# Block attention and a top-1 mixture of experts on one core: value products from three 16-bit passes, gate products by batch

## The chip, the cores and the metric

One of the eight cores of a Trainium2 chip runs the whole kernel. The metric is device time in microseconds; a kernel is run several times and the median counts. The profile is taken in one execution.

## The reference

```python
# q, k, v: (8, 8, 576, 64) f32; 8 batches x 8 heads, 576 tokens, 64 per head
scores = (1/sqrt(64)) * q @ k.T                  # per batch and head
scores = where(pos_i // 64 >= pos_j // 64, scores, -1e9)
attn = exp(scores - max(scores)); attn /= sum(attn) + 1e-9
x = (attn @ v) as (4608 tokens, 512)             # heads side by side
logits = x @ w_gate                              # 8 experts
e = argmax(logits); gate = softmax(logits)[e]; eom = sigmoid(x @ w_output_gate)[e]
out[token] = gate * eom * (relu(x @ w1[e]) @ w2[e])   # w1 (512, 1024), w2 (1024, 512)
```

All results are f32. The choice of the expert hangs on small differences of the logits, so the attention has to be close to f32.

## The kernel before, in words

**Two stages.** The attention goes through 32 pairs of heads (8 batches, 4 pairs each). Its output x goes to DRAM, and after each batch a routing step writes each token's number and weight into a table sorted by expert. The experts' stage then takes groups of up to 256 tokens of one expert: gather x, two layers with w1 and w2 (each number split into two 16-bit parts, three products), scale, scatter to the output.

**One pair.** A class `Pair` has a method for each step; here with their lines.
- `fetch` (L103) loads q and k of both heads into `nat`. `split` (L109, L110) makes of each the upper f16 part and the f16 rest, in two pieces of 320 and 256 elements: the cast is on POOL for k and on ACT for q, the rest on POOL. `turn` (L118) transposes by DMA into `tr`. `highs` copies the upper parts into `kx` and `qx` (L122, L123, both DVE), 64 x 1152 each. `fetch_v` loads V (L129, L130) as f32 into `vf`, with a column of ones behind the 64 columns, so that the value product gives the sum of the probabilities too.
- `max_tile` 0 to 3: scores from upper parts alone, into a double PSUM bank, and their maximum over keys on DVE (L150 for tiles 0 and 1, L155 for 2 and 3; L158 writes them scaled as f16).
- `turn_max`: five transposes (L164), an ACT copy of the maxima into `qx` for the first head (L165), a DVE copy of that for the second (L166).
- `prob_tile` 0 to 3: scores in full, keys on partitions (L176, L177), maximum subtracted by the product itself; ACT takes the exponential (L189) into `pt`, f32, 2304 elements a partition in all.
- `values` 0 and 1, one head each: 15 f32 products of a 128x128 block of `pt` (the stationary operand) with 65 columns of `vf` (L207); then DVE adds 1e-9, inverts and scales (L209 to L211), and two DMAs store x (L216, L217).
- `turn_x`: five f32 transposes (L222, L226), two ACT copies to `xT` (L223, L227). `logits`: five f32 products with the 16 gate columns (L234), added to `L` on DVE (L237, L239).

**Order.** The order of PE is written by hand. Round g = 4p + r issues for r = 0 `max_tile(0)`, `prob_tile(2)` and `turn_x`; for r = 1 `turn_max`, `max_tile(1)`, `prob_tile(3)`, `logits`; for r = 2 and 3 `values(0)` or `values(1)`, then a `prob_tile` and a `max_tile`, each of the pair whose turn it is: probabilities run one pair behind the maxima, values two, x three. A table of events by round issues the loads and splits some rounds ahead (`make` 12, `split` 9 and 8, `turn` 7 and 6, `highs` 3 rounds ahead of the pair's first tile). Other engines take their instructions in an order that the scheduler fixes beforehand, by priority; each engine's queue is worked off in order. All DMAs but the gathers, scatters and table accesses go through SP's queue.

**Routing.** `finish_batch` (L394 to L443) is a generator that goes one step on in each round: the one-hot choice, its rank by products with triangular ones (L408 to L413), softmax and sigmoid on DVE and ACT, the product `z` on POOL (L436), five scatters into the table (L443, POOL). After the last pair, `first_tiles` fills PE with the first expert's products while this runs, one block of 12 products per step; then `route_rest` computes the groups of all other tokens. The first expert's weights are loaded and split on ACT and POOL (`load_first`, L657, L659) during the last pairs.

**PSUM.** Eight banks: `ps_s`, three double banks, for scores; `ps_o`, two single ones, for everything else.

Of the kernel before, what the change touches and what calls it, by code (L numbers as in the profile page):

```python
# [26 lines left out]
def block_attention_top1_moe(  # L27
# [44 lines left out]
    NSET = 4  # L72

# [3 lines left out]
    ps_o = ctx.enter_context(tc.tile_pool(name="ps_o", bufs=2, space=PSUM))  # L77
# [8 lines left out]

    def bank():
        return ps_o.tile([P, 512], F32, name="ps_o")

    class Pair:  # L90
# [22 lines left out]
        def room(self, which):  # L113
            self.tr[which] = sb.tile([P, NR, P], F16, name=f"tr{which}", bufs=5)
            return self.tr[which]
# [4 lines left out]
        def highs(self):  # L120
            self.trk, self.trq = (self.tr[i].rearrange("c r p -> c (r p)") for i in range(2))
            nc.vector.tensor_copy(self.kx[0:64], self.trk[0:64])  # L122
            nc.vector.tensor_copy(self.qx[0:64], self.trq[64:128])  # L123

        def fetch_v(self):
            h0 = 2 * self.hp
            self.v = vfs[self.p % len(vfs)]
            for h in range(2):
                nc.sync.dma_start(self.v[:, h, 0:4, 0:D], v[self.b, h0 + h, 0:512].rearrange("(j p) d -> p j d", p=P))  # L129
            nc.sync.dma_start(self.v[64:128, :, 4, 0:D], v[self.b, h0:h0 + 2, 512:576, :].rearrange("h p d -> p h d"))  # L130

        def max_tile(self, i):
            if i == 0:
                self.nmx = small.tile([P, NT, 2], F32, name="nmx")
            ps = ps_s.tile([P, 2, 512], F32, name="ps_s")
# [7 lines left out]
            if i < 2:  # L143
# [5 lines left out]
                for t, sl in zip(ts, cols):  # L149
                    last_max[0] = nc.vector.tensor_reduce(self.nmx[:, t, :], ps[:, :, sl], AX.X, ALU.max, negate=True)  # L150
            else:
# [3 lines left out]
                last_max[0] = nc.vector.tensor_reduce(self.nmx[:, 4, ab:ab + 1], flat[:, 0:S], AX.X, ALU.max, negate=True)  # L155
            if i == 3:
                self.nmz = nmzs[self.p % 2]
                nc.vector.tensor_scalar(self.nmz[:, :, 96:98], self.nmx, 1.0 / MS, None, ALU.mult)  # L158

        def turn_max(self):  # L160
            pm = ps_o.tile([P, 1024], F16, name="ps_o")
            for t in range(NT):
                at = QS[t] - (64 if 0 < t < 4 else 0)
                nc.tensor.transpose(pm[:, at:at + P], self.nmz[:, t, :], ident16)  # L164
            nc.scalar.copy(self.qx[96:98, 0:S], pm[96:98, 0:S])  # L165
            nc.vector.tensor_copy(self.qx[96:98, S:2 * S], self.qx[96:98, 0:S])  # L166

        def prob_tile(self, i):
            if i == 0:
                self.pt = [sb.tile([P, 2, n], F32, name=f"pt{j}") for j, n in enumerate((S, 512, 512))]  # L170
            ps = ps_s.tile([P, 2, 512], F32, name="ps_s")
# [7 lines left out]
            if i < 2:  # L179
                for ab in range(2):  # L180
                    for o, k0, q0 in (((0, 320), 256, 256), ((320, 512), 384, 384)) if i == 0 else (((0, 448), 128, 128), ((448, 512), 448, 512)):
                        products(ps[:, ab, o[0]:o[1]], ab, k0, q0, o[1] - o[0])
                to, ap = self.pt[2 - i], ps
            else:
                ab = i - 2
                products(flat[:, 0:512], ab, 0, 0, 512)
                products(flat[:, 512:S], ab, 0, 512, 64)
                to, ap = self.pt[0][:, ab], flat[:, 0:S]
            last_exp[0] = nc.scalar.activation(to, ap, AF.Exp, scale=SCALE)  # L189

        def values(self, ab):
            if ab == 0:
                self.xn = sb.tile([P, NT, P], F32, name="xn", bufs=3)
            o = bank()[:, 0:NT * (D + 1)].rearrange("p (t c) -> p t c", c=D + 1)
            p0, p1, p2 = (x[:, ab] for x in self.pt)
            for t in range(NT):
                w = [p0[:, QS[t]:QS[t] + P]]
                if t > 0:
                    w.append(p1[:, QS[t] - 128:QS[t]])
                if t > 1:  # L200
                    w.append(p2[:, QS[t] - 256:QS[t] - 128])
                if t > 2:
                    w.append(p2[:, 320 + QS[t] - 384:320 + QS[t] - 256])
                if t > 3:
                    w.append(p1[:, 384:512])
                for j, wj in enumerate(w):
                    nc.tensor.matmul(o[:, t], wj, self.v[:, ab, j, :], start=(j == 0), stop=(j == len(w) - 1))  # L207
            sm = small.tile([P, NT], F32, name="sm")
            nc.vector.tensor_scalar(sm, o[:, :, D], 1e-9, None, ALU.add)  # L209
            nc.vector.reciprocal(sm, sm)  # L210
            nc.vector.tensor_tensor(  # L211
                self.xn[:, :, ab * D:(ab + 1) * D], o[:, :, 0:D], sm.unsqueeze(2).broadcast_to([P, NT, D]), ALU.mult
            )
            if ab:
                to = x_d[self.b * S:(self.b + 1) * S, self.hp * P:(self.hp + 1) * P]
                nc.sync.dma_start(to[0:512].rearrange("(t p) c -> p t c", p=P), self.xn[:, 0:4])  # L216
                nc.sync.dma_start(to[512:S], self.xn[64:128, 4])  # L217

        def turn_x(self):
            self.xT = sb.tile([P, S], F32, name="xT")  # L220
            pa = bank()
            nc.tensor.transpose(pa[:, 0:P], self.xn[:, 4], ident)  # L222
            nc.scalar.copy(self.xT[:, 512:S], pa[:, 64:P])  # L223
            pa = bank()
            for t in range(4):
                nc.tensor.transpose(pa[:, P * t:P * t + P], self.xn[:, t], ident)  # L226
            nc.scalar.copy(self.xT[:, 0:512], pa)  # L227

        def logits(self):
            if self.hp == 0:  # L230
                logit[self.b] = small.tile([P, NT, 16], F32, name="L")
            o = bank()[:, 0:NT * 16].rearrange("p (t c) -> p t c", c=16)
            for t in range(NT):
                nc.tensor.matmul(o[:, t], self.xT[:, QS[t]:QS[t] + P], wg[:, self.hp, :], start=True, stop=True)  # L234
            L = logit[self.b]
            if self.hp == 0:
                nc.vector.tensor_copy(L, o)  # L237
            else:
                nc.vector.tensor_tensor(L, L, o, ALU.add)  # L239
            if self.hp == NP - 1:  # L240
                later.append(finish_batch(self.b, L))

    logit = {}

    with tc.high_priority(offset=3000):
# [15 lines left out]
        wg = const.tile([P, NP, 16], F32, name="wg")  # L261
# [4 lines left out]
        vfs = [sb.tile([P, 2, NT, D + 1], F32, name=f"vf{i}", bufs=1) for i in range(3)]  # L266
# [32 lines left out]
    def opening():  # L299
# [9 lines left out]
        rest = bank().rearrange("p (a n) -> p a n", n=P)  # L309
        for i in range(2):  # L310
            tr = x.room(i)
            ps = ps_s.tile([P, 2, 512], F32, name="ps_s").rearrange("p a (b n) -> p (a b) n", n=P)
# [17 lines left out]
    with tc.high_priority(offset=1000):  # L330
# [4 lines left out]
        for x in vfs:  # L335
            nc.gpsimd.memset(x[:, :, :, D:D + 1], 1.0)
            nc.gpsimd.memset(x[0:64, :, 4, :], 0.0)
        for i in range(2, NSET):
# [49 lines left out]

    def finish_batch(b, L):

        yield
        lg, lz = L[:, :, 0:E], L[:, :, E:2 * E]
# [12 lines left out]
        )  # L405
        yield
# [29 lines left out]
        nc.gpsimd.tensor_tensor(z, lz, oh, ALU.mult)  # L436
# [5 lines left out]
        for t in range(NT):  # L442
# [9 lines left out]
            scatters.append(sc)  # L452

# [228 lines left out]
    def load_first():  # L682
# [18 lines left out]
        for w, fn, r0, r1 in ((w1, split_w1, 2, 1), (w2, split_w2, 2, 1)):  # L701
# [150 lines left out]
    NPR = B * NP  # L852
# [9 lines left out]
    for p in range(1, NPR):  # L862
# [7 lines left out]
        at(max(base - 3, 2), lambda p=p: pairs[p].highs())  # L870
    for p in range(NPR):
        at(4 * p + 3, lambda p=p: pairs[p].fetch_v())
# [31 lines left out]
    def round_of(g):  # L904
# [10 lines left out]
        if r == 1:  # L915
            do(5, "turn_max")
        do(r, "max_tile", r)
        if r < 2:
            do(8 + r, "prob_tile", 2 + r)
            do(12 + r, ("turn_x", "logits")[r])  # L920
        else:
            do(8 + r, "values", r - 2)
            do(4 + r, "prob_tile", r - 2)
        pay_later()

    NG = 4 * NPR + 10
# [9 lines left out]
    route_rest()  # L936
    for r in ahead:
# [108 lines left out]
```

## Time and profile before

| | |
|---|---|
| three runs | 907.78 us median (896.85 to 940.01) |
| profiled execution | 903.48 us, span 901.9 us |
| mean granted clock of TensorE | 0.958 |
| busy, share of the span | PE 94%, weight loads (PEld) 74%, DVE 60%, ACT 46%, POOL 34% |

The span runs from the first to the last instruction. Attention takes the first 500 us, the experts the rest. Rows of a timeline give start, duration, engine, line, operation and tiles; what stands in brackets is the engine's idle time before the row and what ended it. Matmuls are pipelined: a row's duration is longer than the distance to the next start.

### The profile page before, as it was taken

The numbers are of one execution on the slowest core, as the hardware profiler recorded it, in microseconds if no ns is written. First come the engines' busy times: TensorE is split into PE (matmuls) and PEld (weight loads), VectorE is DVE, ScalarE is ACT, GpSimd is POOL, SyncE is SP. The second block draws the span as 40 slices with busy tenths as digits, with TensorE's granted clock in tenths as the row PEclk, the third lists the DMA queues.
The fourth block names the chain that finished last, engine by engine and source line by source line (L and its number), as shares of the span: only waits on it lengthen the run. The fifth ranks groups of instructions, "written<-read, shape, count | busy, mean of one in ns | idle before, by whom it ended". The sixth has DMA issues, their size and how long they took to land. (4 is left out here: it accounts for less than half of the span.)

```text
span 901.9 us, 18672 instructions
## 1 busy us (share of the span) xinstructions
PE 846.8 (94%) x7144; PEld 664.0 (74%) x7144; DVE 538.2 (60%) x1026; ACT 416.0 (46%) x600; POOL 309.5 (34%) x397
## 2 busy tenths in 40 slices
PE   2899999999999989999799899999999999999995
PEld 1688888888888878888688667677766857586662
DVE  9755656556565653655411628686876867686640
ACT  2344344344344342433332128575756857675540
POOL 7522433425334341320642255552233223321001
PEclk9999999999999996999776799999999999999998
DMA  8966766776975663542520077979999997862511
GB/s 150 180 136 127 138 147 138 147 139 127 150 140 132 138 135 87 113 88 69 181 60 13 15 253 168 352 197 311 290 324 298 353 298 211 262 174 54 178 70 38
DMA packets 274578, 148.46 MB, mean 165 GB/s; under 512 B 228304, under 2 KB 246768, under 8 KB 274480
## 3 DMA queue, kind: packets, MB, share of 16 engines
q1 hardware_dynamic: 266432, 127.89, 57.9%
q0 software_dynamic: 8048, 19.29, 6.4%
q8 instruction: 58, 0.95, 0.5%
q14 instruction: 40, 0.33, 0.2%
HBM read 126.03 MB, written 19.34 MB: 161 GB/s over the span
## 5 line engine op out<-in xcount | busy, mean ns | idle before, releaser
L207 PE MATMUL ps_o<-vf,pt 128*128 128x65 f32 x1920 | 244.7, 289 | 1.2 <-issue 0.5
L207 PEld LDWEIGHTS ps_o<-vf,pt 128*128 128x128 f32 x1920 | 237.4, 205 | 9.9 <-issue 3.2
L189 ACT ACTIVATE pt<-ps_s 128x576 f32<-128x576 f32 (+1 forms) x128 | 105.8, 838 | 227.9 <-PE ps_s L177 195.8
L780 PEld LDWEIGHTS <-w1b 128*128 128x128 f16 (+1 forms) x2208 | 177.7, 98 | 24.0 <-issue 1.4
L780 PE MATMUL ps_s<-xt,w1b 128*128 128x256 f16 (+5 forms) x1920 | 175.3, 253 | 0.4 <-DVE w1b L659 0.3
L809 PE MATMUL ps_o<-w2b,hh 128*128 128x512 f16 (+1 forms) x560 | 166.7, 379 | 0.3 <-issue 0.3
L659 DVE TENSOR_TENSOR w2b<-w2f,w2b 128x1024 bf16<-128x1024 f32 x80 | 92.9, 1222 | 88.6 <-ACT w2b L657 88.1
L110 POOL TENSOR_TENSOR sp<-nat,sp 128x320 f16<-128x320 f32 (+1 forms) x126 | 93.0, 756 | 89.3 <-ACT sp L109 89.0
L150 DVE TENSOR_REDUCE nmx<-ps_s 128x2 f32<-128x896 f32 (+3 forms) x128 | 85.7, 690 | 39.4 <-PE ps_s L139 37.6
L809 PE MATMUL ps_o<-w2b,hl 128*128 128x512 f16 x280 | 106.1, 379 | 0.0
L176 PE MATMUL ps_s<-qx,kx 98*128 98x64 f16 (+4 forms) x384 | 103.4, 290 | 0.0
L818 POOL DMA_INDIRECT out_dram<-ys,ids x38 | 46.4, 1220 | 157.6 <-ACT ys L817 84.6
L809 PEld LDWEIGHTS <-hh 128*128 128x128 f16 x560 | 54.4, 98 | 62.1 <-issue 0.5
L209 DVE TENSOR_SCALAR sm<-ps_o 128x5 f32<-128x5 f32 x64 | 10.6, 165 | 145.0 <-PE ps_o L207 125.4
L659 DVE TENSOR_TENSOR w1b<-w1f,w1b 128x1024 bf16<-128x1024 f32 x80 | 93.2, 1221 | 2.0 <-ACT w1b L657 1.6
L177 PE MATMUL ps_s<-tr,tr 128*128 128x64 f16 (+4 forms) x384 | 89.3, 289 | 0.0
L657 ACT CAST w1b<-w1f 128x1024 f16<-128x1024 f32 x80 | 78.7, 1047 | 4.9 <-DMA w1f<-in_moe_w_dram 4.6
L139 PE MATMUL ps_s<-kx,qx 72*128 72x64 f16 (+4 forms) x384 | 69.8, 295 | 10.3 <-DVE qx L123 6.5
L657 ACT CAST w2b<-w2f 128x1024 f16<-128x1024 f32 x80 | 77.9, 1045 | 1.1 <-DMA w2f<-in_moe_w_dram 0.8
L817 ACT ACTIVATE ys<-ps_o,ids 128x512 f32<-128x512 f32 (+1 forms) x38 | 26.1, 687 | 108.6 <-PE ps_o L809 88.7
L629 POOL DMA_INDIRECT xg<-x_d,ids x38 | 56.3, 1481 | 32.6 <-DMA ids<-tab_d 14.5
L109 POOL CAST sp<-nat 128x320 f16<-128x320 f32 (+1 forms) x60 | 24.7, 438 | 100.9 <-DMA nat<-in_k_dram 73.0
(178 smaller groups left out, 924.7 us busy)
## 6 DMA issues: line engine op xcount, KB each, us to landing
w1f<-in_moe_w_dram SPq DMA_DIRECT2D x80, 512.0 KB
w2f<-in_moe_w_dram SPq DMA_DIRECT2D x80, 512.0 KB
nat<-in_k_dram SPq DMA_DIRECT2D x32, 288.0 KB
nat<-in_q_dram SPq DMA_DIRECT2D x32, 288.0 KB
vf<-in_v_dram SPq DMA_DIRECT2D x64, 128.0 KB
x_d<-xn SPq DMA_DIRECT2D x32, 256.0 KB
hh<-in_moe_w_dram SPq DMA_DIRECT2D x4, 512.0 KB
hl<-in_moe_w_dram SPq DMA_DIRECT2D x4, 512.0 KB
```

Of the source, the lines that this page charges most:

```text
L110: last_lo[0] = lo.tensor_tensor(sp[:, sl, 1 - which, :], self.nat[which][:, sl], sp[:, sl, which, :], ALU.subtract)
L139: nc.tensor.matmul(o, self.qx[0:KM, ab * S + Q0[t]:ab * S + Q0[t] + P], self.kx[0:KM, ab * S + c0:ab * S + c1], start=True, stop=True)
L150: last_max[0] = nc.vector.tensor_reduce(self.nmx[:, t, :], ps[:, :, sl], AX.X, ALU.max, negate=True)
L176: nc.tensor.matmul(o, self.kx[0:KT, ks], self.qx[0:KT, qs], start=True, stop=False)
L177: nc.tensor.matmul(o, self.trk[:, ks], self.trq[:, qs], start=False, stop=True)
L189: last_exp[0] = nc.scalar.activation(to, ap, AF.Exp, scale=SCALE)
L207: nc.tensor.matmul(o[:, t], wj, self.v[:, ab, j, :], start=(j == 0), stop=(j == len(w) - 1))
L629: nc.gpsimd.indirect_dma_start(out=xg[i % NXG][0:width[i], h], out_offset=None, in_=x_d[0:nx, :], in_offset=IOA(ap=ids[i][0:width[i], h, 0 ...
L657: nc.scalar.copy(hi, src)
L659: eng.tensor_tensor(lo[at], src[at], hi[at], ALU.subtract)
L780: nc.tensor.matmul(ph[:, f4].rearrange("p (h n) -> p h n", n=w), wv[:, cc, f, :], xv[:, cc], start=(k == 0), stop=(k == 3 * KD - 1))
L809: nc.tensor.matmul(py, hv[:, f, h], wv[:, f, :], start=(k == 0), stop=(k == 3 * KF - 1))
```

## The change

- **Values.** `pt` stays f32. Its upper 16 bits are read in place as bf16 (every second 16-bit element), and `prob_tile` adds a rest, `pt` minus that upper part, as f16 in `pl`: two of 1024 elements a pair on DVE, two of 576 on POOL (on DVE for the last four pairs). V is split into f16 parts `vh` (ACT) and `vl` (POOL). Each value product becomes three: upper x `vh` (65 columns), upper x `vl` (64), rest x `vh` (65). Both heads' sums lie in a PSUM tile of their own, and are scaled by one set of DVE instructions over both.
- **Gates.** `xT` is kept for a whole batch. `finish_batch` begins with products that have the gate columns (padded to 32) as the stationary operand, the four pairs in four column groups, one ACT copy, five transposes and one DVE reduction over the four groups.
- **`highs`** are two SBUF to SBUF DMAs on SP's queue, issued four rounds ahead instead of three (DVE copies for pair 0 alone). `turn_max` writes both heads by one ACT copy. `z` is on DVE. Maxima have a higher priority on DVE.
- **PSUM.** `ps_s` keeps three double banks and serves everything in the attention; a double bank `ps_v` holds the value sums; `ps_o` is made after the attention.
- **Order.** Values of a pair begin one round after its third probability tile, and rounds 0 and 1 hold the values. `finish_batch` has more steps (gates, transposes, two empty ones, one per scatter). `load_first` waits longer between its blocks.

```diff
     def highs(self):
...
+            if self.p == 0:
+                nc.vector.tensor_copy(self.kx[0:64], self.trk[0:64])
+                nc.vector.tensor_copy(self.qx[0:64], self.trq[64:128])
+            else:
+                nc.sync.dma_start(self.kx[0:64], self.trk[0:64])
+                nc.sync.dma_start(self.qx[0:64], self.trq[64:128])
...
+        def split_v(self):
+            nc.scalar.copy(self.vh[:, :, :, 0:D], self.vn)
+            nc.gpsimd.tensor_tensor(self.vl, self.vn, self.vh[:, :, :, 0:D], ALU.subtract)
...
     def turn_max(self):
...
-            nc.scalar.copy(self.qx[96:98, 0:S], pm[96:98, 0:S])
-            nc.vector.tensor_copy(self.qx[96:98, S:2 * S], self.qx[96:98, 0:S])
+            nc.scalar.copy(
+                self.qx[96:98].rearrange("p (h s) -> p h s", h=2), pm[96:98, 0:S].unsqueeze(1).broadcast_to([2, 2, S])
+            )
...
     def prob_tile(self, i):
...
-            last_exp[0] = nc.scalar.activation(to, ap, AF.Exp, scale=SCALE)
+            last_exp[0] = nc.scalar.activation(self.pt[j][at], ap, AF.Exp, scale=SCALE)
+            (nc.vector if j or self.p >= NPR - 4 else nc.gpsimd).tensor_tensor(self.pl[j][at], self.pt[j][at], self.high(j)[at], ALU.subtract)
+
+        def high(self, j):
+            return self.pt[j].bitcast(BF16)[:, :, 1::2]
...
     def values(self, ab):
...
-                for j, wj in enumerate(w):
-                    nc.tensor.matmul(o[:, t], wj, self.v[:, ab, j, :], start=(j == 0), stop=(j == len(w) - 1))
+                for j in reversed(range(len(w))):
+                    i, c = w[j]
+                    hi, lo = (x[:, ab, c:c + P] for x in (self.high(i), self.pl[i]))
+                    first, last = j == len(w) - 1, j == 0
+                    nc.tensor.matmul(o[:, t], hi, self.vh[:, ab, j], start=first, stop=False)
+                    nc.tensor.matmul(o[:, t, 0:D], hi, self.vl[:, ab, j], start=False, stop=False)
+                    nc.tensor.matmul(o[:, t], lo, self.vh[:, ab, j], start=False, stop=last)
...
     def finish_batch(b, xT):
...
+        for c0, c1 in ((0, 512), (512, S)):
+            for g in range(NP):
+                nc.tensor.matmul(
+                    pm[32 * g:32 * g + 32, c0:c1], wg[:, g, :], xT[:, g, c0:c1],
+                    start=True, stop=True, tile_position=(0, 32 * g),
+                )
+        nc.scalar.copy(lgT, pm[:, 0:S])
+        yield
...
+        for t in range(NT):
+            nc.tensor.transpose(pm[:, t], lgT[:, QS[t]:QS[t] + P], ident)
+        L = small.tile([P, NT, 16], F32, name="L")
+        nc.vector.tensor_reduce(
+            L, pm.rearrange("p t (g c) -> p t c g", c=32)[:, :, 0:16], AX.X, ALU.add
+        )
...
-        nc.gpsimd.tensor_tensor(z, lz, oh, ALU.mult)
+        nc.vector.tensor_tensor(z, lz, oh, ALU.mult)
...
     def round_of(g):
...
+        if r == 0:
+            do(8, "prob_tile", 3)
+            do(12, "turn_x")
+            do(4, "turn_max")
+            do(0, "max_tile", 0)
+            do(8, "values", 0)
+        elif r == 1:
+            do(1, "max_tile", 1)
+            do(5, "prob_tile", 0)
+            do(9, "values", 1)
+        elif r == 2:
+            do(2, "max_tile", 2)
+            do(6, "prob_tile", 1)
+        else:
+            do(3, "max_tile", 3)
+            do(7, "prob_tile", 2)
```

## Rows read from the trace of the kernel before

**Rows 1.** Stretch 200 to 250: busy of PE, PEld, DVE, ACT, POOL; clock, DMA share.
```profile
200.00:250.00 50.00, 49.03 (x443) 42.84 (x443) 29.84 (x82) 18.45 (x34) 22.58 (x34) 1.00 0.76 136
```

**Rows 2.** Timeline of PE, one pair of heads.
```profile
222.51 0.38 PE L176 MATMUL ps_s<-qx,kx 98*128 98x512 f16 x1
...
225.29 1.26 PE L234 MATMUL ps_o<-wg,xT 128*128 128x16 f32 x10
...
226.65 3.54 PE L207 MATMUL ps_o<-vf,pt 128*128 128x65 f32 x30
230.03 0.30 PE L176 MATMUL ps_s<-qx,kx 98*128 98x320 f16 x1
...
235.88 0.38 PE L176 MATMUL ps_s<-qx,kx 98*128 98x512 f16 x1
```

**Rows 3.** A group of weight loads (busy us, mean ns); timeline of 64-column products.
```profile
L207 PEld LDWEIGHTS ps_o<-vf,pt 128*128 128x128 f32 x1920 | 237.4, 205 | 9.9 <-issue 3.2 <-DVE L L239 0.4
...
603.63 0.22 PE L833 MATMUL ps_o<-hh,w2b 128*128 128x64 f16 x2
...
605.46 0.22 PE L833 MATMUL ps_o<-hh,w2b 128*128 128x64 f16 x2
```

**Rows 4.** Groups of DVE by form: busy us, mean ns, idle before.
```profile
L659 DVE TENSOR_TENSOR w1b<-w1f,w1b 128x1024 bf16<-128x1024 f32 x80 | 93.2, 1221 | 2.0 <-ACT w1b L657 1.6
...
L211 DVE TENSOR_TENSOR xn<-ps_o,sm 128x320 f32<-128x320 f32 x64 | 31.4, 491 | 1.8
...
L123 DVE COPY qx<-tr 64x1152 f16<-64x1152 f16 x32 | 19.0, 593 | 1.7 <-DMA tr<-sp 0.7
L150 DVE TENSOR_REDUCE nmx<-ps_s 128x2 f32<-128x384 f32 x32 | 17.8, 557 | 0.9
...
L166 DVE COPY qx<-qx 2x576 f16<-2x576 f16 x32 | 11.7, 365 | 1.0
```

**Rows 5.** Groups of POOL by form.
```profile
L110 POOL TENSOR_TENSOR sp<-nat,sp 128x320 f16<-128x320 f32 x63 | 51.1, 811 | 83.0 <-ACT sp L109 82.9
...
L110 POOL TENSOR_TENSOR sp<-nat,sp 128x256 f16<-128x256 f32 x63 | 44.2, 702 | 6.3 <-ACT sp L109 6.1
L443 POOL DMA_INDIRECT tab_d<-idg,sli x40 | 40.3, 1006 | 32.5 <-DVE nmx L150 15.3 <-issue 9.9 <-DVE sli L427 7.3
...
L109 POOL CAST sp<-nat 128x320 f16<-128x320 f32 x30 | 14.2, 473 | 100.9 <-DMA nat<-in_k_dram 73.0 <-DMA tr<-sp 27.9
```

**Rows 6.** Groups of ACT by form.
```profile
L189 ACT ACTIVATE pt<-ps_s 128x1024 f32<-128x1024 f32 x64 | 65.6, 1024 | 218.4 <-PE ps_s L177 188.8 <-PE ps_s L139 29.7
L189 ACT ACTIVATE pt<-ps_s 128x576 f32<-128x576 f32 x64 | 41.7, 652 | 9.5 <-PE ps_s L177 7.0 <-issue 1.4 <-PE ps_o L226 0.3
```

**Rows 7.** DMA, 200 to 300: packets, MB, share; a stretch: PE, clock, share, GB/s.
```profile
q1 hardware_dynamic: 52022, 14.01, 73.5%
...
30.00:35.00 5.00, 5.00 (x25) 1.00 1.09 203
```

**Rows 8.** Timeline of POOL and DVE, the same DVE line beside POOL and without it.
```profile
203.06 1.42 POOL L110 TENSOR_TENSOR sp<-nat,sp 128x320 f16<-128x320 f32 x2
203.43 0.48 DVE L397 TENSOR_TENSOR eq<-L,mx 128x40 f32<-128x40 f32 x1
...
501.56 0.20 DVE L397 TENSOR_TENSOR eq<-L,mx 128x40 f32<-128x40 f32 x1
```

**Rows 9.** z on POOL; PE's long waits; the stretches behind them, columns as rows 1.
```profile
440.94 0.25 POOL L436 TENSOR_TENSOR z<-L,oh 128x40 f32<-128x40 f32 x1
...
441.82 0.69 PE L164 MATMUL ps_o<-ident,nmz 128*128 128x128 f16 x5 [4.96 <-ACT xT L223]
...
479.82 1.29 PE L234 MATMUL ps_o<-wg,xT 128*128 128x16 f32 x10 [1.67 <-ACT xT L227]
...
445.00:450.00 5.00, 5.00 (x25) 4.72 (x25) 1.04 (x3) 0.94 (x2) 3.86 (x4) 0.50 0.62 165
...
485.00:490.00 5.00, 4.64 (x23) 4.27 (x22) 1.54 (x4) 0.59 (x1) 0.00 (x0) 0.50 0.00 0
```

More of the change, by code (lines that the diff above doesn't have):

```diff
@@ L113, in room @@
         def room(self, which):
[L114 removed]
+            self.tr[which] = sb.tile([P, NR, P], F16, name=f"tr{which}", bufs=4)
             return self.tr[which]
@@ L134, in max_tile @@
                 self.nmx = small.tile([P, NT, 2], F32, name="nmx")
-            ps = ps_s.tile([P, 2, 512], F32, name="ps_s")
+            ps = banks()
             flat = ps.rearrange("p a n -> p (a n)")
@@ L170, in prob_tile @@
                 self.pt = [sb.tile([P, 2, n], F32, name=f"pt{j}") for j, n in enumerate((S, 512, 512))]
-            ps = ps_s.tile([P, 2, 512], F32, name="ps_s")
+                self.pl = [sb.tile([P, 2, n], F16, name=f"pl{j}") for j, n in enumerate((S, 512, 512))]
+            ps = banks()
             flat = ps.rearrange("p a n -> p (a n)")
@@ L191, in values @@
         def values(self, ab):
             if ab == 0:
[L193 to L197, printed above, removed]
+                self.pv = ps_v.tile([P, 2, 512], F32, name="ps_v")
+            o = self.pv[:, ab, 0:NT * (D + 1)].rearrange("p (t c) -> p t c", c=D + 1)
+            for t in reversed(range(NT)):
+                w = [(0, QS[t])]
@@ L219, in turn_x @@
         def turn_x(self):
[L220 to L225, printed above, removed]
-                nc.tensor.transpose(pa[:, P * t:P * t + P], self.xn[:, t], ident)
[L227 to L239, printed above, removed]
+            if self.hp == 0:
+                xTs[self.b] = sb.tile([P, NP, S], F32, name="xT")
@@ L240, in logits @@
+            pa = banks().rearrange("p a n -> p (a n)")
+            for t in range(NT):
+                nc.tensor.transpose(pa[:, P * t:P * t + P], self.xn[:, t], ident)
+            xT = xTs[self.b]
+            nc.scalar.copy(xT[:, self.hp, 0:512], pa[:, 0:512])
+            nc.scalar.copy(xT[:, self.hp, 512:S], pa[:, 576:640])
             if self.hp == NP - 1:
-                later.append(finish_batch(self.b, L))
-    logit = {}
+                later.append(finish_batch(self.b, xT))
+    xTs = {}
@@ L308, in opening @@
         x.split(1, nc.scalar.copy, nc.gpsimd)
-        rest = bank().rearrange("p (a n) -> p a n", n=P)
+        rest = ps_v.tile([P, 2, 512], F32, name="ps_v")[:, 0].rearrange("p (a n) -> p a n", n=P)
         for i in range(2):
             tr = x.room(i)
-            ps = ps_s.tile([P, 2, 512], F32, name="ps_s").rearrange("p a (b n) -> p (a b) n", n=P)
+            ps = banks().rearrange("p a (b n) -> p (a b) n", n=P)
             for r in range(NR):
```

99 lines of the change are left out of this document (58 added, 41 removed).

## The prediction, with its working

> **What bounds the kernel now.** The busy line gives TensorE (PE) 94% of the span and the next engine 60%. That is an average over two stages, so I cut the span into stretches first. In a steady stretch of the attention (200 to 250 us) PE is busy 49.0 of 50 us, VectorE (DVE) 29.8, ScalarE (ACT) 18.5, GpSimd (POOL) 22.6, and the DMA engines have a share of 0.76 [rows 1]. The attention is bound by PE; the experts' stage behind it is not edited but for its bank pool and its beginning. The timeline of PE gives the period: the same score product starts at 222.51 and at 235.88, one pair of heads in 13.37 us. A run of 30 value instructions begins at 226.65 and the next tile at 230.03, 3.38 us, twice a pair: 6.75 us, half the period. The gate product takes what lies between 225.29 and 226.65 but for a small tile of two products (0.25): 1.1 us [rows 2]. The other 13.37 - 6.75 - 1.1 = 5.5 us are scores (twice), transposes and short waits.
>
> **The change on PE.** A value product is now two f32 instructions, 3.38 us / 30 = 112 ns each, with an f32 weight load of 205 ns beside each [rows 2, 3]. It becomes three 16-bit instructions of 64 or 65 columns: 30 products a pair x 3 = 90, with 90 loads. The nearest row is a 64-column 16-bit product of the experts' stage, also with a fresh load each time: from 603.63 to 605.46 lie 21 groups of three, 63 instructions, 29 ns each [rows 3]. 90 x 29 ns = 2.6 us instead of 6.75: 4.1 us less. Two thirds of them read the upper halves in place, that is, they load weights with a stride of two elements, which no row shows. From below 29 ns; from above the 112 ns of the f32 pass: 60 x 112 + 30 x 29 ns = 8.5 us, 1.7 us more than now. I take 29 ns, since the elements read are 16 bits wide as in that row; the other end is a rival.
>
> Gate products: now 4 x 1.1 = 4.5 us per batch of four pairs. Afterwards 576 columns of f32 in each of four column groups, and five transposes. 112 ns for 65 columns bounds an f32 pass by 1.7 ns a column; two passes of 576 are 2.0 us. Four groups one after another take 8 us, all at once 2; the transposes 0.6. So between 0.5 us less and 1 us more per pair; I take 0. PE then needs 13.37 - 4.1 = 9.2 us a pair, waits of today included.
>
> **What takes over.** DVE: 29.84 us in 50 us, which are 3.74 pairs, is 8.0 us a pair now [rows 1]. Gone: two copies into kx and qx (0.59 each, their waits included), the second copy of the maxima (0.37), half the normalisation's instructions (two of 0.49 become one of 640 elements, 0.49 + 320 x 1.04 ns = 0.82; with two short ones 0.5): 2.0. Added: two rests of 1024 elements from two SBUF operands, the form of the expert weights' rest, 2 x 1.22 = 2.44; per batch a reduction of 320 elements, under the 0.56 of 384, and z, 0.2 a pair [rows 4]. 8.0 - 2.0 + 2.6 = 8.6 us.
>
> POOL now: rests 2 x (0.81 + 0.70), casts 0.47 and a shorter one, a quarter of five scatters of 1.0 each: 5.2 us. From 256 to 320 elements a rest grows by 0.11 us, 1.7 ns an element; 576 elements cost 0.81 + 256 x 1.7 ns = 1.25, twice, and V's rest of 640 takes 1.35 [rows 5]: 3.9 more, together 9.1. For the last four pairs the rests of 576 are DVE's (2 x 0.75): 10.1 there, below the period I come to, so nothing.
>
> ACT: 18.45 us over 3.74 pairs is 4.9 [rows 1]. The maxima's copy gets 576 more elements, at most another 0.65; V's cast of 640 lies between the exponentials of 576 and 1024, 0.65 and 1.02, about 0.7; the batch's copy adds 0.2 [rows 6]: 6.4 us.
>
> DMA: 73.5% of 16 engines over 100 us, 7.48 pairs, is 9.8 us of full share per pair. What a burst can reach is seen while the first pairs are loaded, a share of 1.09 [rows 7]: 9.0 us of wall time now. The two copies, 295 KB together, become transfers within SBUF. At 142 GB/s (14.2 MB in those 100 us, all queues) they would add 2.1 us; at the 203 GB/s of the burst 1.5; their rows are longer than most, so 1.0 at best. That makes 10.0 to 11.1 us. They add a wait, too: SP issues them only when both transposes of the pair have landed, and behind them in SP's queue stand the loads of V and of the next q and k and the stores of x. What SP waits there delays those, then the casts on ACT and POOL, and on ACT the exponentials queued behind a cast.
>
> Last, DVE and POOL meet. While POOL works on its rests (203.06 to 204.48) a small DVE operation on two SBUF operands takes 0.48 us; with POOL idle the same line takes 0.20 [rows 8]. Some 0.3 us for each of the two new rests and as much for the small ones: DVE 8.6 + 0.9 = 9.5.
> The Trainium skill (SBUF — State Buffer, "Who interferes with whom") says more: a DVE instruction with two SBUF inputs and a GpSimd instruction that reads SBUF exclude each other for the whole instruction. By that rule the shared port would carry 7.8 us of POOL and 2.4 + 0.4 of DVE, 10.6 us a pair; by the row alone 9.5.
>
> PSUM: scores, maxima and the transposes of x share three double banks, some ten uses a pair. Each holds its products and its reader, 0.65 to 1.3 us, and some waits, about 2.5 together: 10 x 2.5 / 3 = 8.3 us, below the others.
>
> So PE needs 9.2 us at most, the engines that feed it 9.1 to 9.5, DMA 10.0 to 11.1. Queues that work in order don't overlap perfectly: I take 10.8 us. Saving: 32 x (13.37 - 10.8) = 82 us.
>
> **The end of the attention.** z waits on POOL behind rests of weights (440.94); PE waits 4.96 us until 441.82 for an ACT copy that stands behind z's reader, and then has a granted clock of 0.50 for some 22 us, which costs 11 [rows 9]. With z on DVE these 16 us could come back. But a wait of 1.67 us is followed by 0.50 as well [rows 9], and a PE with 1.6 us to spare in each pair will meet more of them. I set the one against the other. The counts for the rest of the routing come after ten blocks of twelve expert products instead of two; 8 x 12 x 256 columns at 29 ns per 64 [rows 3] are 11 us later, most of it beside products that have to be done anyway: between 0 and +11, I take +4. Sum: the profiled execution's 903.5 (span 901.9) - 82 + 4 = 825 us. The median of the three runs lies 4 us above that execution, less than this sum can tell. A difference of under 2% (18 us) is about what a measurement can't tell from none.
>
> **Rivals.**
> Better feeders: the DMA queue stays full, DVE and POOL rarely meet, 9.5 us a pair, and 10 of the 16 us come back: 903.5 - 124 - 10 = 770. For it: DMA is idle a quarter of the time now. Against: it leaves POOL's 9.1 no room.
> SP's new wait rules: 1 to 1.5 us of idle DMA in each pair, 12.3 us: 903.5 - 34 + 4 = 873. For it: everything goes through one queue, in order.
> The strided loads are slow, so that the change doesn't do what it says on PE. At 85 ns on 60 loads nearly nothing is won (60 x 85 + 30 x 29 ns = 6.0 us); at 112 ns the pair grows by 1.7 us, held back by z's 16 us: 903.5 + 54 - 16 = 941; in the middle about 910.
> The slower side: the clock. At 1.2 GHz the scores (about 4 us a pair) cost 8, the value products 90 x 58 ns = 5.2, the rest 2: 15.2 us. It decides if PE's slack gathers in one wait per pair of 1.67 us or more and the clock falls again each time it has risen: 32 x (15.2 - 13.37) = +58, less the 16: 945. Against it: at 15 us PE is no longer starved and the buffers fill.
> On this the Trainium skill (TensorE: Matmul & The Clock Gate, "A second HAM failure mode: psum-queue depth-cycling") has short idles between groups of matmuls make the clock swing; the rows here show a fall only behind single long waits.
>
> **Chances.** Forecast 0.55, better feeders 0.17, SP's wait 0.08, strided loads 0.12, clock 0.08. The range reaches from the better feeders to just short of the strided case, 772 to 890; the forecast's own is 800 to 850. Faster by over 2%: 0.55 + 0.17 + 0.06 = 0.78; within 2%: 0.12; slower: 0.10.
>
> **What would show it.** Right: value products about 29 ns apart, the same score every 10.5 to 11.1 us, PE under 88% busy in the attention, POOL and DVE each above 78%, a DMA share near 0.95. Wrong: a run of 45 value instructions longer than 2.5 us (loads); a granted clock of 0.50 in more than a third of the stage (clock); DMA share falling while SP waits for the transposes; or PE still above 95%.

## The result and the profile after

The kernel after takes 834.6 us, the median of 4 executions (832.5 to 837.9). The kernel before, run beside it, has a median of 923.9 us over 4 (896.9 to 949.3). The ratio is 0.925, 95% interval 0.914 to 0.937: faster, and 10 us above the 825 that was forecast. The ratio sets the four executions against the two faster ones of the kernel before (896.9 and 907.8 us) and leaves its two slow ones (940.0 and 949.3) out. The profiled execution took 837.9 us with a span of 836.3.

First the profile's page after: busy time by engine, then the granted clock and the DMA share in 40 slices (in tenths).
```profile
PE 704.8 (84%) x7933; PEld 507.5 (61%) x7952; DVE 598.0 (72%) x892; ACT 456.9 (55%) x640; POOL 436.8 (52%) x480
...
PEclk9999989989797999979799899999999999999997
DMA  8989989798999989986413959798999989942601
```
Then stretches of it, with the columns of [rows 1]: the stretch shown there, the attention's steady part, one pair from x store to x store, and a pair in which a batch is routed.
```profile
200.00:250.00 50.00, 38.96 (x574) 29.40 (x573) 39.04 (x69) 26.47 (x43) 38.25 (x41) 0.90 0.90 168
60.00:400.00 340.00, 267.66 (x3982) 202.70 (x3982) 270.59 (x484) 184.78 (x297) 249.56 (x270) 0.91 0.91 170
80.09:90.59 10.50, 10.15 (x163) 7.42 (x162) 8.24 (x15) 7.29 (x12) 7.91 (x9) 1.00 0.95 202
202.09:217.06 14.97, 12.26 (x168) 9.47 (x166) 12.03 (x19) 10.09 (x17) 12.93 (x13) 0.87 0.65 123
```
The reader is to see that PE has fallen from 49.0 to 39.0 of 50 us while VectorE rose by 9 and GpSimd by 16, and that DMA went from 0.76 to 0.90. No engine is full on the average. An ordinary pair takes 10.5 us, the routing pair 15.

The value products themselves, the 45 of one head, from PE's timeline:
```profile
207.40 0.19 PE L235 MATMUL ps_v<-vh,pt 128*128 128x65 f16 x1
207.43 0.19 PE L236 MATMUL ps_v<-vl,pt 128*128 128x64 f16 x1
207.45 0.20 PE L237 MATMUL ps_v<-vh,pl 128*128 128x65 f16 x1
...
208.72 0.19 PE L237 MATMUL ps_v<-vh,pl 128*128 128x65 f16 x1
```
And the group of weight loads that read the upper halves (busy us, mean ns):
```profile
L235 PEld LDWEIGHTS <-pt 128*128 128x128 bf16 x960 | 93.9, 103 | 0.0
```
From 207.40 to 208.72 the 45 starts lie 30 ns apart, and the load with a stride takes 103 ns, where the f32 load took 205 [rows 3].

How the span divides is read from SP's x stores, one per pair. Of the kernel before, the first and the last:
```profile
46.75 0.37 SPq L216 DMA_DIRECT2D x_d<-xn  x1
...
495.99 0.36 SPq L216 DMA_DIRECT2D x_d<-xn  x1
```
Of the kernel after, the same two, and between them the two that bound six whole batches:
```profile
48.14 0.38 SPq L249 DMA_DIRECT2D x_d<-xn  x1
...
90.59 0.52 SPq L249 DMA_DIRECT2D x_d<-xn  x1
...
388.77 0.42 SPq L249 DMA_DIRECT2D x_d<-xn  x1
...
426.18 0.37 SPq L249 DMA_DIRECT2D x_d<-xn  x1
```
Between first and last store lie 31 pairs: 449.2 us before, 378.0 after, 71.2 less. The first store comes 1.4 us later. What follows the last one is 405.9 us before (span 901.9) and 410.1 after, 4.2 more. 71.2 - 1.4 - 4.2 = 65.6, the whole difference of the spans.

Neither time is 31 times its ordinary pair. Before: 31 x 13.37 = 414.5, so 34.7 us went into a few long pairs (21.7 and 27.7 us the worst). After, against the forecast pair: 31 x 10.8 = 334.8, so 43.2 us more. The first four pairs, with no routing beside them, take 42.5 (10.6 each); the six whole batches 298.2, 39.0 above 24 x 10.8; the last three pairs 37.4, 5.0 above. **In each of the six batches that is one long pair of 15 to 16.5 us and one of 11.5 to 12, and in four of them one more of 12.7 to 13.1**; it is what the experiments are about.

The routing pair of the kernel after (start, duration, instruction), first GpSimd's timeline:
```profile
202.86 2.19 POOL L212 TENSOR_TENSOR pl<-pt 128x576 f16<-128x576 f32 x1 [3.64 <-ACT pt L211]
205.02 1.36 POOL L145 TENSOR_TENSOR vl<-vn,vh 128x640 f16<-128x640 f32 x1
206.34 1.14 POOL L212 TENSOR_TENSOR pl<-pt 128x576 f16<-128x576 f32 x1
207.64 1.01 POOL L488 DMA_INDIRECT tab_d<-idg,sli  x1 [0.16 <-DVE nmx L166]
...
212.40 1.06 POOL L488 DMA_INDIRECT tab_d<-idg,sli  x1 [0.32 <-issue]
213.44 0.82 POOL L115 CAST sp<-nat 128x320 f16<-128x320 f32 x2
214.19 1.43 POOL L116 TENSOR_TENSOR sp<-nat,sp 128x320 f16<-128x320 f32 x2
```
VectorE's in the same microseconds:
```profile
202.84 1.22 DVE L212 TENSOR_TENSOR pl<-pt 128x1024 f16<-128x1024 f32 x1
203.97 1.11 DVE L470 SCALAR_TENSOR_TENSOR sl<-er,rank 128x5 f32<-128x5 f32 x1
205.11 1.29 DVE L472 TENSOR_SCALAR sli<-sl 128x5 int32<-128x5 f32 x1
```
And SP's queue, three rows that follow each other:
```profile
209.28 0.89 SPq L109 DMA_DIRECT2D nat<-in_q_dram  x1
215.65 1.32 SPq L124 DMA_TRANSPOSE tr<-sp  x1
217.06 0.58 SPq L249 DMA_DIRECT2D x_d<-xn  x1
```
Two things stand here. Four scatters run one after another from 207.64 to 213.46, and k's split waits behind them; its transpose leaves SP only at 215.65, after 5.5 us in which SP issues nothing, and the x store that ends this pair stands behind it (so sums over whole batches say more than a single pair). And the three VectorE rows follow GpSimd's: an operation on five elements that begins at 203.97 ends at 205.08, as GpSimd's rest ends (205.05); the next ends at 206.40, as GpSimd's V rest does (206.38).

What SP and PE themselves wait for, from 60 to 400 us of the kernel after (us in total, turns, the longest):
```profile
SPq L124 <- POOL sp L116: 50.0, 16, 7.9
PE ps_v L237 <- POOL pl L212: 15.6, 8, 3.8
PE ps_s L257 <- DVE xn L245: 14.2, 7, 3.3
```
SP stands for GpSimd's splits. PE's two longest sums are for GpSimd's rests, that is in the value products, and for VectorE's normalised x; a wait for a transpose or for the transfers into `kx` and `qx` is not among PE's longer ones.

### The profile page after: what moved, and what is told of

Read it like the earlier page. It is cut to its first block, busy times and chain, and to the rows that moved or that the text cites. A ratio compares the mean times of both kernels' runs of the same rounds, so it can differ in the third digit from the quotient of the medians.

```text
span 836.3 us, 20367 instructions
## 1 busy us (share of the span) xinstructions
PE 704.8 (84%) x7933; PEld 507.5 (61%) x7952; DVE 598.0 (72%) x892; ACT 456.9 (55%) x640; POOL 436.8 (52%) x480
## 5 line engine op out<-in xcount | busy, mean ns | idle before, releaser
L237 PE MATMUL ps_v<-vh,pl 128*128 128x65 f16 x960 | 105.5, 201 | 29.3 <-POOL pl L212 15.6
L166 DVE TENSOR_REDUCE nmx<-ps_s 128x2 f32<-128x896 f32 (+3 forms) x128 | 81.5, 683 | 60.0 <-PE ps_s L154 60.0
L212 DVE TENSOR_TENSOR pl<-pt 128x1024 f16<-128x1024 f32 (+1 forms) x72 | 103.7, 1446 | 20.7 <-ACT pt L211 20.7
L237 PEld LDWEIGHTS <-pl 128*128 128x128 f16 x960 | 93.3, 102 | 31.5 <-POOL pl L212 17.5
L235 PE MATMUL ps_v<-vh,pt 128*128 128x65 f16 x960 | 106.3, 202 | 0.0
L236 PE MATMUL ps_v<-vl,pt 128*128 128x64 f16 x960 | 106.0, 200 | 0.0
L212 POOL TENSOR_TENSOR pl<-pt 128x576 f16<-128x576 f32 x56 | 80.7, 1456 | 44.9 <-ACT pt L211 44.9
L116 POOL TENSOR_TENSOR sp<-nat,sp 128x320 f16<-128x320 f32 x126 | 96.4, 790 | 14.8 <-ACT sp L115 14.7
L154 PE MATMUL ps_s<-kx,qx 72*128 72x64 f16 (+4 forms) x384 | 73.0, 306 | 25.1 <-DVE nmx L166 9.6
L235 PEld LDWEIGHTS <-pt 128*128 128x128 bf16 x960 | 93.9, 103 | 0.0
L236 PEld LDWEIGHTS <-pt 128*128 128x128 bf16 x960 | 93.7, 104 | 0.0
```

What stands on the lines that cost most here:

```text
L116: last_lo[0] = lo.tensor_tensor(sp[:, sl, 1 - which, :], self.nat[which][:, sl], sp[:, sl, which, :], ALU.subtract)
L212: (nc.vector if j or self.p >= NPR - 4 else nc.gpsimd).tensor_tensor(self.pl[j][at], self.pt[j][at], self.high(j)[at], ALU.subtract)
L235: nc.tensor.matmul(o[:, t], hi, self.vh[:, ab, j], start=first, stop=False)
L236: nc.tensor.matmul(o[:, t, 0:D], hi, self.vl[:, ab, j], start=False, stop=False)
L237: nc.tensor.matmul(o[:, t], lo, self.vh[:, ab, j], start=False, stop=last)
```

## The experiments

In the accounts below, "six batches" is the time from the fifth x store to the twenty-ninth, after: 298.2 us. "Whole" is a single time where no median is named.

**Without the scatters** of the first six batches (their tokens stay out of the table):
```
+            if b < 6:
+                yield
+                continue
             sc = nc.gpsimd.indirect_dma_start(
```


> The kernel after without the five scatters of the table of tokens for batches 0 to 5 (these tokens stay out of the table; the attention alone is read). Theory A (GpSimd's in-order queue: the scatters stand between rests and casts, and the routing pairs lose 6 to 9 us a batch by that): the four-pair sums of x stores fall from 48-51 us to 43-45 us, the last x store comes 25 to 40 us earlier (from 426 to 386-400 us), VectorE's small routing operations come back near 0.4-0.6 us. Theory B (the routing's small operations on VectorE themselves and what PE waits for them): sums stay within 2 us, last x store 415-426. Theory C (half-clock stretches behind a long PE wait): half of the gain of A, and the mean clock of 60 to 400 us rises above 0.95 only if the waits go with the scatters.

Six batches 272.5, the last store at 399.4, 26.8 us earlier: theory A, at the low end. A routing pair of it, as a stretch:
```profile
240.11:252.08 11.97, 8.87 (x140) 6.62 (x138) 11.87 (x18) 8.14 (x13) 10.90 (x11) 1.00 0.99 182
```
VectorE is busy 11.87 of 11.97 us. The part of A on VectorE's small operations fell: they don't get shorter without the scatters. These rows of the same run, from 60 to 400 us, are the two longest of them:
```profile
L470 DVE SCALAR_TENSOR_TENSOR sl<-er,rank 128x5 f32<-128x5 f32 x7 | 15.1, 2162 | 0.0
L472 DVE TENSOR_SCALAR sli<-sl 128x5 int32<-128x5 f32 x7 | 7.9, 1130 | 0.2
PE ps_v L237 <- POOL pl L212: 1.4, 2, 0.9
```
The mean of the first is one operation of 8.49 us in the seventh batch, which the kernel after has too (further down); the other six take 1.11 us, as they do there. The sums of four pairs, 42.8 to 47.0 us, came down less far than A's 43 to 45. The third row is PE's wait for GpSimd's rests: 1.4 us instead of 15.6, so that is a way by which the scatters reach PE. So 25.7 of the 39.0 us belong to the scatters. For the other 13.3, VectorE, held up by GpSimd's rests, is what this stretch shows full; that was not tested by itself.

**Without V's loads** from the third pair on (those pairs work on old values, so the routing and the experts' time differ; the attention alone counts):
```
+            if self.p >= 2:
+                return
             h0 = 2 * self.hp
```


> The kernel after with V loaded for the first two pairs only (30 pairs work on old values of V, their loads are left out). Theory A (an ordinary pair is bound by the DMA queue, share 0.91 to 1.0): some 288 of 1,700 KB a pair go, the ordinary pair falls from 10.5 to about 9.0-9.5 us, the last x store comes 30 to 50 us earlier. Theory B (bound by VectorE and GpSimd, which hold each other up): DMA share falls to 0.75-0.8, the period stays within 0.3 us, the last x store within 10 us.

First four pairs 40.3 instead of 42.5, six batches 311.2, the last store at 427.4; the DMA share from 60 to 400 us is 0.75. So theory A fails for the stage: a sixth of the DMA load gone buys nothing there, and 0.55 us in each of the first four pairs. Why the routing pairs grew (up to 22.0 us) isn't settled; perhaps V's split, with no load to wait for, takes another place beside the rests.

**k's and q's copies on VectorE again:**
```
-            if self.p == 0:
+            if True:
                 nc.vector.tensor_copy(self.kx[0:64], self.trk[0:64])
```


> The kernel after with the two copies of k's and q's upper halves on VectorE again for every pair, instead of transfers within SBUF. Theory A (DMA bounds the pair): 1.0 to 1.5 us of DMA a pair go, VectorE gets 0.8 to 1.2 us, the ordinary pair stays at 10.5 or falls to 10.0; last x store 405-426. Theory B (VectorE and GpSimd bound it): the pair grows by 0.8 to 1.2 us, last x store 445 to 465.

```profile
60.00:400.00 340.00, 258.01 (x3578) 194.76 (x3578) 256.10 (x472) 168.00 (x271) 247.64 (x257) 0.85 0.66 131
```
Last store at 456.4, first four pairs 48.1: 1.4 us more a pair, the whole 867.9. DMA has dropped to 0.66 and it helps nothing. Theory B. Making the copies transfers was worth about 30 us.

**All rests on VectorE**, none on GpSimd:
```
-            (nc.vector if j or self.p >= NPR - 4 else nc.gpsimd).tensor_tensor(self.pl[j][at], ...
+            nc.vector.tensor_tensor(self.pl[j][at], ...
```


> The kernel after with the two rests of 576 elements a pair on VectorE in every pair, instead of GpSimd. GpSimd gets 2.5 to 3 us a pair free, VectorE 1.5 to 2.4 us more. Theory A (GpSimd's in-order queue delays the splits of q and k and with them the transposes): the ordinary pair falls to 9.5-10, and the routing pairs lose less: last x store 395 to 415. Theory B (VectorE is the bound, by its own work and the shared port): the pair grows by 0.5 to 1.5 us, last x store 435 to 465. Theory C (DMA bounds it): within 8 us of 426.

Last store at 408.4, six batches 284.9, first four pairs 41.5; whole 817.9. VectorE goes to 314.8 of 340 us and the kernel is faster: in the routing pairs GpSimd's queue was the nearer bound. Theory A, with ordinary pairs hardly shorter. What is left in its trace are two waits of PE:
```profile
PE ps_v L237 <- DVE pl L212: 23.1, 15, 8.5
PE ps_s L257 <- DVE xn L245: 22.6, 7, 3.8
```
The 8.5 us of the first belong to the seventh batch; its others are 1.4 us at most.

**k's upper cast on ScalarE** instead of GpSimd:
```
-pairs[p].split(0, nc.gpsimd.tensor_copy, nc.gpsimd)
+pairs[p].split(0, nc.scalar.copy, nc.gpsimd)
```


> The kernel after with k's upper cast on ScalarE instead of GpSimd: GpSimd 0.6 to 0.9 us a pair less, ScalarE 0.6 more. Theory A (GpSimd's in-order queue sets the routing pairs, as the runs with rests or scatters taken off it suggest, 2.5 us a pair there for 18 us in all): the last x store comes 5 to 12 us earlier than 426. Theory B (the rests' place in the order counts, not GpSimd's load): within 4 us. Theory C (the cast delays the exponentials on ScalarE): 5 to 15 us later.

Last store at 436.1, 10 us later, and the whole 847.3: theory C's number. But 8.5 of the 10 us are in the last three pairs (45.9 us instead of 37.4), beside the loading of the first expert's weights; the six batches are 300.2, 2.0 more, as theory B had it. C's delayed exponentials are not shown. GpSimd's load alone is not the cause: from 60 to 400 us it is busy 24 us less (225.5), and no batch is won by it.

**The normalisation ahead of the rests**, on the kernel with all rests on VectorE:
```
+            with tc.high_priority(offset=60):
                 nc.vector.tensor_scalar(sm, o[:, :, :, D], 1e-9, None, ALU.add)
                 nc.vector.reciprocal(sm, sm)
                 nc.vector.tensor_tensor(self.xn...
```


> The kernel with all rests on VectorE, and in addition the normalisation of x (three VectorE operations) given the same priority as the maxima, so that the rests don't stand between its parts. With the rests on VectorE, PE waited 22.6 us in seven turns for xn. Theory A (that wait is what is left of the routing pairs' loss, and the half clock follows it): the wait goes below 5 us, the last x store from 408 to 385-398. Theory B (the time goes to the rests that are late instead, PE waits for pl): the last x store stays within 404-412.

The wait for xn falls from 22.6 us to 0.4. Last store at 401.0, six batches 275.0, whole 812.8: between A and B, 7.4 us earlier than without. An ordinary and a routing pair of it:
```profile
182.32:192.41 10.09, 8.33 (x142) 6.43 (x141) 10.09 (x30) 6.01 (x11) 4.59 (x7) 1.00 1.01 208
237.28:251.63 14.35, 10.78 (x184) 8.25 (x181) 12.22 (x19) 7.27 (x11) 12.85 (x13) 1.00 0.90 152
```
In the first VectorE is busy all 10.09 us and DMA is full beside it; in the second GpSimd is at 12.85 of 14.35.

**Two value passes instead of three** (upper halves by V's rest are left out from the third pair on):
```
+                    if self.p < 2:
                         nc.tensor.matmul(o[:, t, 0:D], hi, self.vl[:, ab, j], start=False, stop=False)
```


> The kernel after without the second of the three value passes (upper halves by V's rest) from the third pair on: 30 products a pair, 0.9 us of PE at full clock, are left out. Theory A (PE is no longer what the pairs wait for): the last x store stays within 422-428, the ordinary pair at 10.5 us. Theory B (PE's own chain still sets part of it): 15 to 28 us earlier. Theory C (the shorter groups give more idle time and more stretches at half clock): later than 428, with a lower mean clock than 0.91 from 60 to 400 us.

Last store at 420.6, six batches 297.2 (after: 298.2), whole 837.1, clock 0.84 from 60 to 400 us instead of 0.91. Near A (the store is 1.4 us below its range), with C's lower clock. But the test is weaker than it was meant to be: 26 us of products at full clock are gone, and PE's busy time from 60 to 400 us falls by only 5.9 us, to 261.8, since the lower clock takes the rest back. It doesn't show what fewer products at an equal clock would bring.

**The kernel before with z on VectorE**, one part of the change alone:
```
-        nc.gpsimd.tensor_tensor(z, lz, oh, ALU.mult)
+        nc.vector.tensor_tensor(z, lz, oh, ALU.mult)
```


> The kernel before with one part of the change alone: z of the routing on VectorE instead of GpSimd. Theory A (the prediction's 16 us: z on GpSimd behind rests of weights makes PE wait at the end of the attention and half the clock follows): 10 to 20 us less than the kernel before in the same rounds, in the trace no PE wait over 1 us between the last x store and the experts, no stretch at half clock there. Theory B (the wait only moves to another operation of the routing): within 6 us.

Medians 925.9 us (10 executions, 905.6 to 939.9) and 929.5 for the kernel before (13, 906.1 to 947.7): the fastest differ by 0.5 us and the medians by 3.6, which with such a spread is nothing that can be told. The trace says more. PE's timeline at the end of this run's attention, with its two waits of over 1 us:
```profile
452.75 0.44 PE L164 MATMUL ps_o<-ident,nmz 128*128 128x128 f16 x5 [1.44 <-ACT xT L223]
...
488.81 1.29 PE L234 MATMUL ps_o<-wg,xT 128*128 128x16 f32 x10 [1.67 <-ACT xT L227]
```
Two stretches behind them, columns as [rows 1]:
```profile
460.00:465.00 5.00, 5.00 (x25) 4.19 (x24) 1.31 (x4) 0.89 (x1) 4.38 (x6) 0.50 0.56 138
...
495.00:500.00 5.00, 4.64 (x22) 4.27 (x23) 1.54 (x4) 0.59 (x1) 0.00 (x0) 0.50 0.00 0
```
The wait of 4.96 us [rows 9] is gone, and the last three pairs take 55.1 us instead of 60.7: 5.6 of the forecast 16 us. Behind each of the shorter waits the granted clock is 0.50 again, and from 440 to 520 us it is 0.74 in the mean (before: 0.70). What follows the last store is the same, 406.7 us against 405.9. So theory B, in the main: shorter waits go on at the same copies.

**The scatters one round later each**, on two kernels:
```
             scatters.append(sc)
             yield
+            if b < B - 1:
+                yield
```


> The kernel with all rests on VectorE and the normalisation ahead of them, and the five scatters of each of the first seven batches issued every second round instead of every round, so that fewer of them fall into one pair. Theory A (in the routing pair GpSimd's queue is full, 12 to 13.5 of 13.3 to 16.7 us, and in the other pairs it has 4 us to spare): the routing pair falls to 11-13 us, the batch from 45.1-47.6 to 42-44.5, the last x store from 401 to 380-392. Theory B (VectorE, busy 9.8 to 11.2 us in every pair, takes over at once): batch 44.5 to 46, the last x store 394-401. Theory C (scatters later in the queue delay the splits of the next pairs as much): within 4 us of 401.

> The kernel after with nothing changed but the scatters' rounds: every second one instead of every one. Leaving the scatters out gained 27 us. Theory A (it is the five in a row that cost): 10 to 20 us of it come back, the last x store at 406-416. Theory B (GpSimd's whole load in a batch sets it): within 6 us of 426.

Last stores at 404.9 and 426.1, whole 818.1 and 837.7. Neither test tells: in both traces four of the five scatters still stand together (on the second at 207.58, 208.89, 211.03 and 212.31, within 0.1 us of those after). Asking for a later round did not change the order on GpSimd.

**An order edge for each scatter**, behind a split that was issued before it:
```
+            if b < B - 1:
+                tc.add_manual_dep(sc, last_lo[0].ins.name, NOSYNC, reason="between the splits")
+                yield
             yield
```


> The kernel with all rests on VectorE and the normalisation ahead of them, and now an order edge on GpSimd: each scatter of the first seven batches stands behind a split of q or k that was issued before it, so that three fall into one pair and two into the next (asking for later rounds alone had left four of the five together). Theory A (GpSimd's queue, full in the routing pair, delays the splits and so the transposes): the routing pair falls from 13.3-16.7 to 11-13 us, the last x store from 401 to 383-395, the whole to 793-805. Theory B (VectorE, 9.5 to 10.5 us of work in every pair and 1 to 1.5 us more beside the routing, is the bound by now): the last x store at 396-403, the whole at 808-815. Theory C (each scatter blocks as long wherever it stands, and the routing's results come later): later than 403.

Now they are apart: 201.64, 205.76, 209.37, 215.38 and 218.15 us. Median 824.2 us (4 executions, 821.0 to 828.5), ratio to the kernel before 0.907, interval 0.895 to 0.918; last store at 417.3. Theory C: spread between splits they lengthen two pairs (11.6 to 16.5, then in five of six batches 14.2 to 15.5 us) instead of one. PE's longest wait now:
```profile
PE ps_s L155 <- DMA qx<-tr: 20.2, 8, 5.5
```
That is the wait by way of SP that the prediction had as a rival: the transpose late, q's copy behind it late, and the scores late.

**All scatters behind both splits of a pair**, three in one pair and two in the next:
```
+            if b < B - 1 and t in (0, 3):
+                for _ in range(4):
+                    yield
...
+                tc.add_manual_dep(sc, last_lo[0].ins.name, NOSYNC, reason="behind the splits")
```


> The kernel with all rests on VectorE and the normalisation ahead of them; the scatters of the first seven batches are held until both splits of a pair are done and stand before V's rest, three in one pair and two in the next. There GpSimd waits 4.5 to 6.5 us for V's cast on ScalarE in most pairs (188.5 to 193 us of the attention in all). Theory A (a scatter costs where a split, and so a transpose, stands behind it): the pairs of 13.3 to 16.7 us fall to 11-12.5, the batch from 45-47.6 to 42.5-44.5, the last x store from 401 to 380-392, the whole to 790-803. Theory B (VectorE's load with the routing's small operations is the bound): the batch 44.5-46, the last x store 395-401, the whole 805-813. Theory C (V's rest late behind the scatters makes the value products wait): later than 403.

(What the expectation gives for GpSimd's wait is a slip: in that kernel it waits 56.8 us for V's cast from 60 to 400 us, in fourteen turns.) Median 819.9 us (4 executions, 812.6 to 823.9), ratio 0.895, interval 0.881 to 0.909: the fastest that was timed over several executions, and all four lie below the four of the kernel after (832.5 to 837.9). It is no gain over the kernel without the edges, whose single time is 812.8. None of the theories holds in full. The pair with three scatters is at 10.8 to 12.7 us, as A had it; the one behind it takes 9.8 to 16.7, and six batches are 278.7, no less than the 275.0 without the edges. In one of the long ones PE stands as here:
```profile
268.79 1.03 PE L155 MATMUL ps_s<-kx,qx 72*128 72x448 f16 x4 [3.39 <-DMA qx<-tr]
```
SP issued that transfer at 262.59; it lands 6 us later, in a pair whose DMA share is 1.10. There the transfers within SBUF and the loads seem to meet. It is not the rule: from 60 to 400 us PE has two such waits, 4.8 us together, and what else lengthens the other pairs isn't settled.

## Why the prediction held, step by step

**Value products: right.** 30 ns apart against 29; strided loads cost nothing that the rows show (103 ns, as much as the loads of the rests without a stride, 102). The rival of the slow loads is out. Its upper end was added up wrongly: 60 x 112 + 30 x 29 ns are 7.6 us, not 8.5, so 0.8 us more a pair than before, and its 941 should have been 914.

**The ordinary pair: right in size.** 10.8 was forecast; the first four pairs take 10.6, later ones 10.0 to 11.0. PE is at 79% from 60 to 400 us (under 88 asked), VectorE at 80% (over 78), DMA at 0.91. GpSimd at 73% missed its 78: it waits 41.7 us of the 340 for the exponentials before its rests, and its rest of 576 elements takes 1.14 us alone (1.25 estimated).

What ends this pair is not one thing. PE isn't full: in the first four pairs it is busy 35.9 of 42.45 us at a granted clock of 1.00 (the run with two passes doesn't settle more). Less DMA gave 0.55 us, more VectorE took 1.4, GpSimd's rests moved to VectorE gave 0.25, k's cast moved off GpSimd gave nothing. The sum of ports that the Trainium skill (SBUF — State Buffer, "Who interferes with whom") led to came to 10.6 us, which is the pair measured, and GpSimd's and VectorE's timelines of the routing pair agree with it for single instructions: VectorE's small operation ends with GpSimd's, however long that takes, and not 0.3 us late as I had taken from [rows 8]. [rows 8] had said so already: its row of 1.42 us holds two rests, and the first alone is
```profile
203.06 0.79 POOL L110 TENSOR_TENSOR sp<-nat,sp 128x320 f16<-128x320 f32 x1
```
It ends at 203.85, and the VectorE operation that began at 203.43 at 203.91. But 0.3 us each and a full DMA queue give the same length for the pair, and no run separates the two. With all rests on VectorE the same sum of ports is only 9.6 us (GpSimd 7.8 - 2.5, VectorE 2.8 + 1.5, an estimate from the prediction's terms) and the pair was 10.4, so there something else ends it: VectorE is busy 314.8 of 340 us.

**The step that was missing: the routing of each batch.** I let it ride in the averages (a quarter of five scatters per pair) and priced only its end. In an in-order queue five scatters are not 1.3 us a pair, four of them are a block of some 6 us in front of a split and of the next pair's rests. The routing cost 39 us over six batches, 25.7 of it shown to be the scatters'. How the block costs it is shown in part: PE's wait for the rests behind it goes with the scatters (15.6 us to 1.4), and SP's wait for the splits falls (50.0 us to 17.7); a way over a late transpose to late scores is not seen in PE's waits of the kernel after. Taking the block out of the splits' way, by order edges, did not bring the time back. The kernel before had room for the block: there GpSimd was busy 123.5 us from 60 to 400, and its batches take 53.5 to 54.5 us except where the clock fell.

**z and the clock: right to set against each other, and lucky in the rest.** z alone gave 5.6 of the 16 us at the end of the attention, because shorter waits are followed by 0.50 as well, as the prediction had feared. The kernel before loses 34.7 us to long pairs, behind z and also in the middle, where the clock is 0.50 from 335 to 355 us behind this wait:
```profile
333.15 0.44 PE L164 MATMUL ps_o<-ident,nmz 128*128 128x128 f16 x5 [2.20 <-ACT xT L223]
```
I had counted only the part behind z. The long pairs after, 43.2 us, have another cause and took their place; that the two nearly cancel is luck. So the saving in the attention is 31 x 2.57 = 79.7 less 8.5, which is 71.2. In the same pair as z's wait, beside the seventh batch's routing, the kernel after has the longest wait of PE in its attention:
```profile
399.95 2.55 POOL L705 TENSOR_TENSOR w1b<-hh,w1b 128x256 bf16<-128x256 f32 x4
...
406.28 2.53 POOL L705 TENSOR_TENSOR w1b<-hh,w1b 128x256 bf16<-128x256 f32 x4
400.34 8.50 DVE L470 SCALAR_TENSOR_TENSOR sl<-er,rank 128x5 f32<-128x5 f32 x1
410.65 0.24 PE L237 MATMUL ps_v<-vh,pl 128*128 128x65 f16 x1 [9.08 <-DVE pl L212]
```
GpSimd works on rests of weights (and one of V) without a gap from 399.95 to 408.81, VectorE's operation on five elements ends at 408.84, and the rest that PE needs stands behind it. The granted clock is 0.55 from 410 to 415 us and 1.00 from 415 to 420.

**The end: right in size.** +4 forecast for what follows the last store, 4.2 measured. It was a value taken from between 0 and +11, and no run takes its parts apart.

**Rivals.** SP's new wait: small after (SP's waits for the transposes' landing are 8.2 us of 340), but it is the wait that came up when the scatters were spread. The clock: 0.91 from 60 to 400 us; two routing pairs at full clock (14.99 and 15.12 us) are nearly as long as those at 0.82 and 0.81 (15.96 and 16.52), so it costs a batch 1 to 1.5 us and isn't the cause.

## What to carry over

When a change takes a third off the bounding engine, price every burst on the engines behind it as a block in their queues, not by its average: what was hidden in the old period can show in the new one. Before moving work between engines, look at which of them holds up the others' order: work moved onto the busiest engine of the stage (VectorE, 270.6 of 340 us) made this kernel faster, and a cast moved off GpSimd won nothing.

## What was not expected of the hardware

- A VectorE operation on 128 x 5 elements takes 0.17 us alone (at 437.27) and 1.11 beside one of GpSimd's on SBUF (203.97); it ends when that ends. Beside a row of thirteen GpSimd operations without a gap it took 8.50 us (400.34). VectorE's rest of 1024 elements is 1.22 us alone and 1.53 in the mean; GpSimd's rest of 576 went from 1.14 to 2.19 us when both started together (202.84 and 202.86).
- A granted clock of 0.50 came behind PE waits of no more than 1.44 and 1.67 us, and stayed while PE was busy all of its time (460 to 465 us).
- Taking a sixth of the load off DMA engines that showed a share of 0.91 (0.75 afterwards) bought 0.55 us in each of the first four pairs and nothing over the stage, where the routing pairs grew.
